# Attention, mixing and gating on one Trainium2 core: the two-bank score tile becomes two tiles of a bank

## The chip, the cores and the metric

The kernel runs on one core of a Trainium2 chip. The metric is the device time of one execution in microseconds, as the median of three runs. The engines are named as the profile names them: PE (TensorE, matmuls), PEld (its weight loads), DVE (VectorE), ACT (ScalarE), POOL (GpSimd) and SP (the queue that issues most DMAs).

## What is computed

Three stages follow each other. The change touches the first alone: attention for 4 batches of 8 heads, 576 positions of 64 features, with a mask in blocks of 64.

```python
scores = scale * np.matmul(q, k.transpose(0, 1, 3, 2))
mask = block_i >= block_j                      # block = 64 positions
scores = np.where(mask, scores, -1000000000.0)
scores = scores - np.max(scores, axis=-1, keepdims=True)
attn = np.exp(scores)
attn = attn / (np.sum(attn, axis=-1, keepdims=True) + 1e-09)
return np.matmul(attn, v).astype(np.float32)
```

The second stage (`_moe_ref`) mixes each position with the one before it and applies three weight matrices; its matmuls write the tiles M. The third (`_moe2_ref`) is a gated layer that mixes positions with a 576 x 576 matrix. All data are float32.

## The kernel before

**Stages and units.** Attention is cut into units. A unit "D" is the low part of one head: queries 0 to 255. A unit "H" is a pair of heads: queries 256 to 511 of each, and the 64 last queries of both heads together, the *tail*, which see all 576 keys. The order (L800) is 16 D units of batches 0 and 1, their 8 H units, then 16 D and 8 H units of batches 2 and 3. The second stage's matmuls (`moe1`, L1295) are woven in between by a schedule of shares (L1375 to L1450), and from about 430 us on the third stage follows alone. In the time line the D units of batches 0 and 1 lie in the first 62 us, the H units of batches 0 and 1 up to about 225 us, the D units of batches 2 and 3 up to about 282 us, and their H units up to about 425 us.

**Scores.** Every unit writes its scores into PSUM. `low_S` (L910) uses 384 columns (128 and 256) of one bank, S0 for even units and S1 for odd ones (for the first four also two tiles M). `high_S` (L1002), called for each head of a pair, writes 384 columns into S0 and 512 into S1. `tail_S` (L1024) writes 576 columns, 288 into the end of the first bank and 288 into the start of the second, so that one instruction can read all 576 side by side. S0 and S1 are the two halves of one tile `sbig` of 1024 columns, which is two banks (L710, L711).

**Softmax.** `soft` (L880) takes a list of parts, each with a column index `c`, the scores in PSUM and the place of the result. For each part DVE copies the scores times -0.125 and keeps the minimum in `nb[:, c]` (`red`, L886), and then ACT takes the exponential from PSUM with that as its bias and adds up the row in `sums` (`exp`, L891). `inverse` (L900) adds the sum and a small constant and takes the reciprocal, and `scaled` (L904) multiplies the probabilities. They are then transposed by TensorE into the tiles T (two tiles of a bank, T0 and T1, L712), and ACT and DVE read them out as a high and a low part (PH, PL) for the product with the values (tiles O0 and O1).

In the profile the first half of an fp32 matmul and the second are two records. P is the probabilities of all parts but the tail, whose tile is Pt.

**How the order is set.** No instruction is emitted where it is written. `nc` is a planner (class `Plan`, L324): every operation is noted with what it reads and writes, and `play` (L402) lays the operations out engine by engine in the order of a modelled time, taking the ready operation of the highest rank. `emit` (L572) then hands them in that order to the framework, which sets the semaphores. For a tile in PSUM the planner notes which banks each operation touches, and lets two engines' operations follow each other where they share a bank (L353 to L360):

```python
lo, hi = x.off // 512, (x.off + sum(st * (n - 1) for st, n in x.dims)) // 512
```

`mm` (L677) also makes the first matmul of a group wait for the last matmul of the group before it in the same tile. `ptile` (L647) hands out a PSUM tile by its tag. Before it reuses one, `order.need` lets the reads of the last use come first in the program's order; `BANKS` (L661) extends this from S to S0 and S1 and back. Where the planner expects TensorE to stand idle in the attention stage, it lays in matmuls on zeros (`calm`, into O0).

All instructions go through `emit` and so carry line 582 in the profile; they are told apart by the names of their tiles.

Of the kernel before, what the change touches and what calls it, by code (L numbers as in the profile page):

```python
# [9 lines left out]
F32 = mybir.dt.float32  # L10
F32R = mybir.dt.float32r
I32 = mybir.dt.int32
AF = mybir.ActivationFunctionType
ALU = mybir.AluOpType
AX = mybir.AxisListType
# [3 lines left out]
B, H, S = 4, 8, 576  # L19
DM = 512  # L20
HF = S // 2
# [8 lines left out]
class Order:  # L30
# [12 lines left out]
    def pe(self, ns):  # L43
        self.run(self.t)
        self.t += ns

    def at(self, dt, fn, *keys):

        heapq.heappush(self.heap, (self.t + dt, self.n, fn))
        for k in keys:  # L50
            self.due[k] = max(self.due.get(k, 0.0), self.t + dt)
        self.n += 1
# [576 lines left out]
def fused_kernel(ctx: ExitStack, tc: tile.TileContext, low, high, tails, mu,  # L629
                 w_k, w_v, w_r, w_in, g_ln, w_sgT, b_sg, w_out, outT):  # L630
    nc = plan = Plan(tc)
# [3 lines left out]
    order = Order()  # L635
# [5 lines left out]
    def pool(name, **kw):  # L641
        p = Pool(plan, name, **kw)
        return p, p

    ring = {}

    def ptile(tag, cols, bufs):  # L647

        r = ring.setdefault(tag, [])
        if len(r) >= bufs:  # L650
            order.need(r[-bufs])
        key = ("ps", tag, len(r))
        r.append(key)
        if tag in fixed:
            t = fixed[tag][(len(r) - 1) % bufs]
            for x in BANKS.get(tag, ()):
                order.need(*ring.get(x, ())[-2:])
            return t, key
        return ps([128, cols], F32, tag, bufs), key

    BANKS = dict(S=("S0", "S1"), S0=("S",), S1=("S",))  # L661


    att_over = []
# [1 line left out]
    def mtile1(w):  # L666
        if att_over:
            tag = att_over[0]
            att_over.append(att_over.pop(0))
        else:  # L670
            tag = "M"
        t, key = ptile(tag, 512, PS_BUFS[tag])
        return t[:, 0:w], key
# [3 lines left out]
    def mm(out, lhsT, rhs, start=False, stop=False):  # L677
        op = nc.tensor.matmul(out=out, lhsT=lhsT, rhs=rhs, start=start, stop=stop)
        t = out.tile
        if start and t in stopped:  # L680
            op.preds[stopped[t].n] = stopped[t]
        if stop:
            stopped[t] = op
# [10 lines left out]
    def sub(who, out, a, b):  # L694
# [12 lines left out]
    x2d = [dram([4, 128, S], F32, f"x2d{b}") for b in range(B)]  # L707

    pcm, ps = pool("ps1", space=PSUM)
    out_ps, sbig = [ps([128, 512], F32, f"O{i}") for i in range(2)], ps([128, 1024], F32, "S")  # L710
    fixed = dict(O=out_ps, S=[sbig], S0=[sbig[:, 0:512]], S1=[sbig[:, 512:1024]],  # L711
                 T=[ps([128, 512], F32, f"T{i}") for i in range(2)])  # L712
    plan.fill(1500.0, "tensor", "matmul", out=out_ps[0][0:64, 512 - FILL:512], lhsT=calm[:, 0:64], rhs=calm, start=True, stop=True)
    mcm, mtile = pool("moe1")
    acm, atile = pool("attn", side="right")

    sums = atile([128, 4, 5, 2], F32, "sums")
    nc.gpsimd.memset(sums[:, :, :, 1], 1e-9)
    ssum = [sums[:, i] for i in range(4)]
    junk = atile([128, 8], F32, "junk")  # L720

# [41 lines left out]
    def w_pair(key, scale, ptile):  # L763

        v = w1[key]
        hi, lo = w1[key] = ptile()
        nc.scalar.activation(out=hi, in_=v, func=AF.Copy, scale=scale)
        if scale != 1.0:
            nc.vector.scalar_tensor_tensor(out=lo, in0=v, scalar=scale, in1=hi.bitcast(F32),
                                           op0=ALU.mult, op1=ALU.subtract)  # L770
        else:
            sub("wl", lo, v, hi.bitcast(F32))
# [107 lines left out]
    def soft(n, parts, normal):  # L880

        sm = ssum[n % 4]
        nb = atile([128, 5], F32, "nb", 4)
        keys = [k for *_, ks in parts for k in ks]

        def red():  # L886
            for c, st, p, _ in parts:
                nc.vector.tensor_scalar(out=p, in0=st, scalar1=-0.125, scalar2=None, op0=ALU.mult, op1=ALU.min,
                                        accum_out=nb[:, c:c + 1])

        def exp():  # L891
            for c, st, p, _ in parts:
                nc.scalar.activation(out=p, in_=st, func=AF.Exp, scale=0.125, bias=nb[:, c:c + 1], accum_out=sm[:, c, 0:1])

        w = sum(st.cols for _, st, _, _ in parts)
        at(0, plan.rank(SB, red), *keys)
        at(1.1 * w + 100, plan.rank(SB, exp), *keys, ("P", n))
        at(2.3 * w + 500, plan.rank(SB, normal), ("P", n))

    def inverse(n, cs, rr):  # L900
        nc.vector.tensor_reduce(out=rr[:, cs], in_=ssum[n % 4][:, cs], axis=AX.X, op=ALU.add)
        nc.vector.reciprocal(out=rr[:, cs], in_=rr[:, cs])

    def scaled(p, r):  # L904
        plan.add(*[("scalar", "activation", dict(out=p, in_=p, func=AF.Copy, scale=r)) if w == "A" else
                   ("vector", "tensor_scalar", dict(out=p, in0=p, scalar1=r, scalar2=None, op0=ALU.mult,
                                                    op1=ALU.add, accum_out=junk[:, 0:1]))
                   for w in WHO["P"]])

    def low_S(n):  # L910
        q, k, v = raws[n]
        tag = SEATS[n] if n < len(SEATS) else f"S{n % 2}"
        st, key = ptile(tag, 512, PS_BUFS[tag])
        p = probs[n] = atile([128, 384], F32, "P2", P2_BUFS)
        pe(4 * 384 / 2.4 + 8)
        parts = []
        b, h = units[n][1:]
        order.need(("sp", n))
        for c, (o, e) in enumerate(((0, 128), (128, 256))):
            qs = slice(128 * c, 128 * c + 128)  # L920
            if b in SCORE_PAIRS:
                Q, K = splits[n]
                mm(st[:, o:o + e], Q[:, qs], K[:, 0:e], start=True)
                mm(st[:, o:o + e], q2[h % 2][:, qs], k2[h % 2][:, LOW:LOW + e], stop=True)
            else:
                mm(st[:, o:o + e], q[:, qs], k[:, 0:e], start=True, stop=True)
            parts.append((c, st[:, o:o + e], p[:, o:o + e], [key]))
        splits.pop(n, None)
        rr = scales[n] = atile([128, 5], F32, "rr", 4)

        def normal():
            inverse(n, slice(0, 2), rr)
            if b in VALUE_PAIRS:
                for c, _, pc, _ in parts:
                    scaled(pc, rr[:, c:c + 1])

        soft(n, parts, normal)
# [64 lines left out]
    def high_S(n, x):  # L1002
        order.need(("sp", n, x))
        Q, K = splits.pop((n, x))
        (s0, k0), (s1, k1) = ptile("S0", 512, 1), ptile("S1", 512, 1)
        p = probs[n, x] = atile([128, 384], F32, "P2", P2_BUFS), atile([128, 512], F32, "P3", P3_BUFS)
        pe(2 * (cost(384) + cost(512)))
        parts = []
        for c, (st, key, e) in enumerate(((s0, k0, 384), (s1, k1, 512))):
            mm(st[:, 0:e], Q[:, 128 * c:128 * c + 128], K[:, 0:e], start=True)  # L1010
            mm(st[:, 0:e], q2[x][:, 128 * c:128 * c + 128], k2[x][:, 0:e], stop=True)
            parts.append((2 * x + c, st[:, 0:e], p[c], [key]))
        if not x:
            scales[n] = atile([128, 5], F32, "rr", 4)
        rr = scales[n]

        def normal():
            inverse(n, slice(2 * x, 2 * x + 2), rr)
            for c in range(2):
                scaled(p[c], rr[:, 2 * x + c:2 * x + c + 1])  # L1020

        soft(n, parts, normal)

    def tail_S(n):  # L1024
        k, q = raws.pop((n, "t"))
        st, key = ptile("S", 1024, 1)
        st = st[:, 512 - HF:512 + HF]
        p = probs[n, "t"] = atile([128, S], F32, "Pt", PT_BUFS)
        pe(8 * HF / 2.4 + 8)
        for i in range(2):  # L1030
            mm(st[:, HF * i:HF * i + HF], q, k[:, HF * i:HF * i + HF], start=True, stop=True)
        rr = scales.pop(n)

        def normal():
            inverse(n, slice(4, 5), rr)
            scaled(p, rr[:, 4:5])

        soft(n, [(4, st, p, [key])], normal)

    def high_T(n, j):  # L1040
        order.need(("P", n))
# [71 lines left out]
    def fronts(n):  # L1113
        if units[n][0] == "D":
            return [lambda: low_S(n)]
        return [lambda: high_S(n, 0), lambda: high_S(n, 1), lambda: tail_S(n)]
# [250 lines left out]
    k = 0  # L1367
# [52 lines left out]
    for i, x in moe1():  # L1420
# [5 lines left out]
        i = ready  # L1426
# [23 lines left out]
        if x > STARTS[-2] + X0_AT * (STARTS[-1] - STARTS[-2]) and not XHL:  # L1450
            XHL[0] = wtile([128, 2, 4, S], F32R, "XHL")
            for f, tag in enumerate(("xh", "xl")):
                t = mtile([128, 4, HF], F32, tag, 2)
# [5 lines left out]
    pcm, ps = pool("ps2", space=PSUM, after=[pcm])  # L1459
# [280 lines left out]
```

## Time and profile before

| what | value |
|---|---|
| median of 3 runs | 707.8 us (707.37 to 709.29) |
| profiled execution | 706.74 us |
| its span (first to last instruction) | 705.0 us |
| PE busy | 681.0 us, 97% of the span |
| PEld busy | 622.6 us, 88% |
| DVE busy | 472.4 us, 67% |
| ACT busy | 420.4 us, 60% |
| POOL busy | 259.2 us, 37% |
| chain that ended last | PE 79%, DVE 7%, ACT 7% |

A busy share is an average over stretches with different limits, so the stretches have to be looked at one by one. Idle time of an engine counts where that engine sets the end. A matmul's end is modelled, and matmuls run one into the other, so PE's busy time also holds some time in which it did less than it could. A line such as "PE S <- ACT P" says that PE stood idle before an instruction that writes S, until an instruction of ACT that writes P had ended.

### The profile page before, as it was taken

The numbers are of one execution on the slowest core, as the hardware profiler recorded it, in microseconds if no ns is written. First come the engines' busy times: TensorE is split into PE (matmuls) and PEld (weight loads), VectorE is DVE, ScalarE is ACT, GpSimd is POOL, SyncE is SP. The second block draws the span as 40 slices with busy tenths as digits, with TensorE's granted clock in tenths as the row PEclk, the third lists the DMA queues.
The fourth block names the chain that finished last, engine by engine and source line by source line (L and its number), as shares of the span: only waits on it lengthen the run. The fifth ranks groups of instructions, "written<-read, shape, count | busy, mean of one in ns | idle before, by whom it ended". The sixth has DMA issues, their size and how long they took to land.

```text
span 705.0 us, 12415 instructions
## 1 busy us (share of the span) xinstructions
PE 681.0 (97%) x4321; PEld 622.6 (88%) x4321; DVE 472.4 (67%) x1321; ACT 420.4 (60%) x1057; POOL 259.2 (37%) x289
## 2 busy tenths in 40 slices
PE   8898999999999888899999999999999999999998
PEld 7777878788999777798999999999898998998997
DVE  4785889777777776687788875771898256346233
ACT  5788786767975787779977886680552132032120
POOL 3004556537741433645645452340235032022031
PEclk9999999999999999999999999999999999999999
DMA  8848132332222222432323214221910400400102
GB/s 309 271 129 287 33 93 83 102 96 68 80 72 82 65 58 87 128 123 82 109 85 120 86 53 155 82 67 46 341 45 4 132 1 0 135 2 6 62 1 68
DMA packets 37403, 67.84 MB, mean 96 GB/s; under 512 B 6564, under 2 KB 21924, under 8 KB 37340
## 3 DMA queue, kind: packets, MB, share of 16 engines
q1 hardware_dynamic: 37196, 67.04, 29.1%
q8 instruction: 34, 0.56, 0.3%
q14 instruction: 29, 0.24, 0.1%
q10 hardware_dynamic: 144, 0.00, 0.0%
HBM read 55.50 MB, written 9.44 MB: 92 GB/s over the span
## 4 chain that ended last, share of the span: by engine, by line
PE 79%; DVE 7%; ACT 7%; DMA 2%; issue 2%; POOL 1%; SPq 0%; ACTq 0%; POOLq 0%; DVEq 0%
PE M L582 37%; PE O L582 16%; PE S L582 12%; PE T L582 7%; PE V L582 7%; ACT P L582 4%; DVE P L582 3%; DVE wv L582 1%; DMA qkv<-high_dram 1%; DVE Pt L582 1%; DVE xT L582 1%; ACT V L582 1%; ACT otmp L582 1%; ACT R L582 1%; DMA q<-Q 1%
## 5 line engine op out<-in xcount | busy, mean ns | idle before, releaser
L582 DVE TENSOR_SCALAR_CACHE_REDUCE P<-S 128x128 f32<-128x128 f32 (+2 forms) x124 | 60.3, 492 | 41.2 <-PE S L582 19.7
L582 PE MATMUL M<-xh,wv 128*128 128x256 f32 (+2 forms) x320 | 85.6, 368 | 0.2
L582 ACT ACTIVATE P<-S,nb 128x128 f32<-128x128 f32 (+2 forms) x124 | 65.3, 528 | 33.4 <-DVE P L582 17.7
L582 DVE TENSOR_TENSOR PL<-T,PH 128x384 fp32r<-128x384 f32 (+1 forms) x128 | 63.2, 505 | 29.0 <-ACT PH L582 23.4
L582 ACT ACTIVATE PH<-T 128x384 fp32r<-128x384 f32 (+3 forms) x152 | 65.2, 432 | 25.6 <-PE T L582 23.4
L582 PE MATMUL M<-xh,w 128*128 128x384 f32 (+1 forms) x272 | 77.6, 340 | 0.0
L582 PE MATMUL M<-kh,wv 128*128 128x320 f32 (+2 forms) x256 | 71.4, 347 | 0.0
L582 PE MATMUL T<-ident,P 128*128 128x128 f32 x320 | 68.8, 279 | 2.4 <-ACT P L582 0.7
L582 POOL TENSOR_TENSOR gt<-gt,U 128x288 f32<-128x288 f32 x32 | 30.9, 970 | 105.7 <-DVE gt L582 55.0
L582 PEld LDWEIGHTS M<-xh,wv 128*128 128x128 f32 x320 | 57.2, 193 | 4.3 <-ACT kl L582 0.3
L582 POOL TENSOR_TENSOR kl<-R,kh 128x384 fp32r<-128x384 f32 (+1 forms) x40 | 41.7, 1044 | 47.3 <-ACT kh L582 45.0
L582 POOL TENSOR_TENSOR xl<-t,xh 128x384 fp32r<-128x384 f32 (+1 forms) x40 | 38.9, 978 | 52.0 <-ACT xh L582 51.7
L582 DVE TENSOR_SCALAR_CACHE_REDUCE P<-P,rr 128x384 f32<-128x384 f32 (+1 forms) x96 | 56.1, 584 | 1.0
L582 ACT ACTIVATE U<-M 128x288 f32<-128x288 f32 x32 | 13.2, 412 | 71.6 <-PE M L582 71.6
L582 PEld LDWEIGHTS T<-ident,P 128*128 128x128 f32 x320 | 42.3, 141 | 13.5 <-DVE P L582 3.4
L582 PE MATMUL O<-gh,w 128*128 128x288 f32 x256 | 52.1, 296 | 0.1
L582 PE MATMUL M<-XHL,w 128*128 128x288 f32 x384 | 51.7, 295 | 0.0
L582 PEld LDWEIGHTS M<-XHL,w 128*128 128x128 f32 x384 | 51.2, 188 | 0.1
L582 PEld LDWEIGHTS M<-xh,w 128*128 128x128 f32 x272 | 49.2, 190 | 1.1
L582 POOL TENSOR_TENSOR V<-qkv,V 128x320 fp32r<-128x320 f32 (+1 forms) x48 | 35.0, 741 | 40.4 <-ACT V L582 35.8
L582 PE MATMUL O<-PH,V 128*128 128x320 f32 (+3 forms) x192 | 48.6, 305 | 0.7 <-ACT PH L582 0.5
L582 PE MATMUL M<-kl,wv 128*128 128x256 f32 (+2 forms) x160 | 47.6, 350 | 0.0
(214 smaller groups left out, 1899.7 us busy)
## 6 DMA issues: line engine op xcount, KB each, us to landing
qkv<-high_dram SPq DMA_DIRECT2D x32, 544.0 KB
tail<-tails_dram SPq DMA_DIRECT2D x16, 352.0 KB
X<-x2d SPq DMA_DIRECT2D x4, 1152.0 KB
outT_dram<-o SPq DMA_DIRECT2D x32, 144.0 KB
w<-w_k_dram SPq DMA_DIRECT2D x4, 1024.0 KB
w<-w_v_dram SPq DMA_DIRECT2D x4, 1024.0 KB
w<-w_in_dram SPq DMA_DIRECT2D x4, 1024.0 KB
qkv<-low_dram SPq DMA_DIRECT2D x20, 132.0 KB
```

What stands on the lines that cost most here:

```text
L582: getattr(getattr(self.nc, e), fn)(*pos, **{k: real(x) for k, x in a.items() if k[0] != "_"})
```

## The change

S0 and S1 become two PSUM tiles of 512 columns, and the tile of 1024 columns goes, with the table `BANKS` and its `order.need`. `tail_S` writes 288 columns at the start of each of the two. Its softmax has two parts for one, with column indices 4 and 5: two reductions, a minimum of the two results into column 4, two exponentials that both take column 4 as their bias, and two row sums, which `inverse` adds up together. `nb` and `sums` get a sixth column, and the small constant of the sixth is zero, with a memset of its own.

```diff
--- before.py
+++ after.py
@@ -653,12 +653,8 @@
         r.append(key)
         if tag in fixed:
             t = fixed[tag][(len(r) - 1) % bufs]
-            for x in BANKS.get(tag, ()):
-                order.need(*ring.get(x, ())[-2:])
             return t, key
         return ps([128, cols], F32, tag, bufs), key
-
-    BANKS = dict(S=("S0", "S1"), S0=("S",), S1=("S",))
 
 
     att_over = []
@@ -707,15 +703,16 @@
     x2d = [dram([4, 128, S], F32, f"x2d{b}") for b in range(B)]
 
     pcm, ps = pool("ps1", space=PSUM)
-    out_ps, sbig = [ps([128, 512], F32, f"O{i}") for i in range(2)], ps([128, 1024], F32, "S")
-    fixed = dict(O=out_ps, S=[sbig], S0=[sbig[:, 0:512]], S1=[sbig[:, 512:1024]],
+    out_ps = [ps([128, 512], F32, f"O{i}") for i in range(2)]
+    fixed = dict(O=out_ps, S0=[ps([128, 512], F32, "S0")], S1=[ps([128, 512], F32, "S1")],
                  T=[ps([128, 512], F32, f"T{i}") for i in range(2)])
     plan.fill(1500.0, "tensor", "matmul", out=out_ps[0][0:64, 512 - FILL:512], lhsT=calm[:, 0:64], rhs=calm, start=True, stop=True)
     mcm, mtile = pool("moe1")
     acm, atile = pool("attn", side="right")
 
-    sums = atile([128, 4, 5, 2], F32, "sums")
-    nc.gpsimd.memset(sums[:, :, :, 1], 1e-9)
+    sums = atile([128, 4, 6, 2], F32, "sums")
+    nc.gpsimd.memset(sums[:, :, 0:5, 1], 1e-9)
+    nc.gpsimd.memset(sums[:, :, 5, 1], 0.0)
     ssum = [sums[:, i] for i in range(4)]
     junk = atile([128, 8], F32, "junk")
 
@@ -880,17 +877,22 @@
     def soft(n, parts, normal):
 
         sm = ssum[n % 4]
-        nb = atile([128, 5], F32, "nb", 4)
+        nb = atile([128, 6], F32, "nb", 4)
         keys = [k for *_, ks in parts for k in ks]
+
+        halves = parts[0][0] == 4
 
         def red():
             for c, st, p, _ in parts:
                 nc.vector.tensor_scalar(out=p, in0=st, scalar1=-0.125, scalar2=None, op0=ALU.mult, op1=ALU.min,
                                         accum_out=nb[:, c:c + 1])
+            if halves:
+                nc.vector.tensor_tensor(out=nb[:, 4:5], in0=nb[:, 4:5], in1=nb[:, 5:6], op=ALU.min)
 
         def exp():
             for c, st, p, _ in parts:
-                nc.scalar.activation(out=p, in_=st, func=AF.Exp, scale=0.125, bias=nb[:, c:c + 1], accum_out=sm[:, c, 0:1])
+                d = min(c, 4)
+                nc.scalar.activation(out=p, in_=st, func=AF.Exp, scale=0.125, bias=nb[:, d:d + 1], accum_out=sm[:, c, 0:1])
 
         w = sum(st.cols for _, st, _, _ in parts)
         at(0, plan.rank(SB, red), *keys)
@@ -898,7 +900,8 @@
         at(2.3 * w + 500, plan.rank(SB, normal), ("P", n))
 
     def inverse(n, cs, rr):
-        nc.vector.tensor_reduce(out=rr[:, cs], in_=ssum[n % 4][:, cs], axis=AX.X, op=ALU.add)
+        x = ssum[n % 4][:, cs] if cs.start < 4 else ssum[n % 4][:, 4:6].rearrange("p (a c) t -> p a (c t)", a=1)
+        nc.vector.tensor_reduce(out=rr[:, cs], in_=x, axis=AX.X, op=ALU.add)
         nc.vector.reciprocal(out=rr[:, cs], in_=rr[:, cs])
 
     def scaled(p, r):
@@ -1023,19 +1026,21 @@
 
     def tail_S(n):
         k, q = raws.pop((n, "t"))
-        st, key = ptile("S", 1024, 1)
-        st = st[:, 512 - HF:512 + HF]
         p = probs[n, "t"] = atile([128, S], F32, "Pt", PT_BUFS)
         pe(8 * HF / 2.4 + 8)
+        parts = []
         for i in range(2):
-            mm(st[:, HF * i:HF * i + HF], q, k[:, HF * i:HF * i + HF], start=True, stop=True)
+            st, key = ptile(f"S{i}", 512, 1)
+            hs = slice(HF * i, HF * i + HF)
+            mm(st[:, 0:HF], q, k[:, hs], start=True, stop=True)
+            parts.append((4 + i, st[:, 0:HF], p[:, hs], [key]))
         rr = scales.pop(n)
 
         def normal():
             inverse(n, slice(4, 5), rr)
             scaled(p, rr[:, 4:5])
 
-        soft(n, [(4, st, p, [key])], normal)
+        soft(n, parts, normal)
 
     def high_T(n, j):
         order.need(("P", n))
```

## Rows read from the trace of the kernel before

**Rows 1.** stretches, us; PE, PEld, DVE, ACT, POOL busy us (instructions); clock; DMA; GB/s
```profile
0.00:75.00 75.00, 65.55 (x473) 55.39 (x474) 48.67 (x166) 53.93 (x146) 16.55 (x36) 0.98 0.71 236
75.00:225.00 150.00, 148.10 (x866) 127.38 (x865) 118.28 (x338) 111.50 (x284) 77.99 (x72) 1.00 0.25 80
225.00:300.00 75.00, 65.97 (x412) 57.70 (x412) 53.55 (x226) 58.85 (x181) 31.18 (x46) 1.00 0.29 87
300.00:425.00 125.00, 124.78 (x761) 115.26 (x761) 101.04 (x305) 107.71 (x278) 67.54 (x69) 1.00 0.29 93
425.00:705.00 280.00, 276.55 (x1816) 266.85 (x1815) 150.88 (x289) 88.39 (x172) 65.90 (x67) 1.00 0.21 71
175.00:200.00 25.00, 24.92 (x172) 23.20 (x171) 19.39 (x61) 24.39 (x66) 17.93 (x23) 1.00 0.34 113
```

**Rows 2.** TensorE's waits, 0 to 75 us: total us, times, longest
```profile
PE S L582 <- ACT P L582: 3.4, 5, 1.0
PE S L582 <- DVE P L582: 1.8, 3, 0.7
```

**Rows 3.** TensorE's waits, 225 to 300 us
```profile
PE S L582 <- ACT P L582: 5.3, 12, 0.8
PE S L582 <- DVE P L582: 2.5, 5, 0.7
```

**Rows 4.** timeline, first high heads: start, us, engine, operation [idle before <-ended by]
```profile
65.78 0.50 PE L582 MATMUL S<-k,q 128*128 128x512 f32 x1 [0.66 <-DVE P L582]
...
69.40 0.56 DVE L582 TENSOR_SCALAR_CACHE_REDUCE P<-S 128x384 f32<-128x384 f32 x1 [0.82 <-PE S L582]
...
70.02 0.50 PE L582 MATMUL S<-k,q 128*128 128x512 f32 x1 [0.66 <-DVE P L582]
...
70.56 0.58 ACT L582 ACTIVATE P<-S,nb 128x384 f32<-128x384 f32 x1 [0.46 <-PE S L582]
```

**Rows 5.** timeline in the low heads of batch 2
```profile
236.94 0.47 ACT L582 ACTIVATE P<-S,nb 128x256 f32<-128x256 f32 x1
...
237.54 0.92 PE L582 MATMUL S<-qkv 66*128 66x128 f32 x4 [0.20 <-ACT P L582]
...
241.26 0.42 DVE L582 TENSOR_SCALAR_CACHE_REDUCE P<-S 128x256 f32<-128x256 f32 x1 [0.57 <-PE S L582]
...
241.75 0.70 PE L582 MATMUL S<-qkv 66*128 66x256 f32 x2 [0.53 <-DVE P L582]
```

**Rows 6.** timeline, the transposes' tiles T in the same stretch
```profile
252.53 0.56 DVE L582 TENSOR_TENSOR PL<-T,PH 128x384 fp32r<-128x384 f32 x1
...
252.66 0.27 PE L582 MATMUL T<-ident,P 128*128 128x128 f32 x1
```

**Rows 7.** stretches around the fall of the granted clock, as rows 1
```profile
64.00:69.00 5.00, 3.35 (x32) 2.49 (x29) 1.46 (x6) 3.36 (x10) 2.99 (x4) 1.00 0.84 255
...
70.30:73.90 3.60, 3.60 (x17) 3.09 (x16) 3.31 (x11) 1.80 (x5) 2.08 (x3) 0.53 0.12 26
```

**Rows 8.** groups by form: count | busy us, mean ns | idle before
```profile
L582 ACT ACTIVATE P<-S,nb 128x256 f32<-128x256 f32 x30 | 14.2, 472 | 8.9 <-PE S L582 6.3 <-DVE P L582 2.6
...
L582 DVE TENSOR_SCALAR_CACHE_REDUCE P<-S 128x256 f32<-128x256 f32 x30 | 12.5, 417 | 5.3 <-ACT P L582 3.4 <-PE S L582 1.8
...
L582 DVE TENSOR_REDUCE rr<-sums 128x2 f32<-128x4 f32 x64 | 9.9, 155 | 20.2 <-ACT P L582 19.3
...
L582 DVE TENSOR_SCALAR_CACHE_REDUCE Pt<-S 128x576 f32<-128x576 f32 x16 | 12.0, 749 | 1.0 <-PE S L582 0.9
L582 ACT ACTIVATE Pt<-S,nb 128x576 f32<-128x576 f32 x16 | 11.8, 737 | 4.5 <-DVE Pt L582 4.4
...
L582 ACT ACTIVATION_READ_ACCUMULATOR Pt<-S,nb 128x1 f32 x16 | 3.1, 192 | 0.0
```

**Rows 9.** waits of the whole run, the weight loads ahead of S
```profile
PEld S L582 <- ACT P L582: 14.6, 30, 1.1
...
PEld S L582 <- DVE P L582: 6.9, 9, 1.0
```

## The prediction

> **What bounds the kernel now.** I read the table of stretches first [rows 1]. From 425 us on TensorE is busy for 276.6 of 280 us (most of the rest is the last output's way out) and in the last attention stretch (300 to 425) for 124.8 of 125, so whatever TensorE loses ahead of that is lost to the end. It loses it in two places: 9.5 us of idle in the first 75 us and 9.0 us between 225 and 300, where the low halves (units of kind "D") of batches 2 and 3 run. DVE (53.6 of 75) and ACT (58.9 of 75) are not full there.
>
> The list of TensorE's waits says for what it stands idle: for the score tile S. Ended by ACT's or DVE's work on P, it is 5.2 us in the first 75 us [rows 2] and 7.8 us in 225 to 300 [rows 3]. P is written from S, so at first sight the bank is simply not read out yet.
>
> The timeline tells more. At 69.40 DVE reduces the 384 columns of S0; the matmul that adds into the 512 columns of S1 starts at 70.02, as that reduction ends, after 0.66 us of idle; and ACT's exponential of S0, whose maximum has been there since 69.96, starts at 70.56, when the matmul into the *other* bank is through [rows 4]. In a low stretch the same: the unit whose scores went in at 237.54 sits in one bank. The next unit's bank was read for the last time by the exponential of 236.94, yet its second matmul waits until 241.75, for the reduction at 241.26, which reads the first unit's bank [rows 5]. So S0 and S1 take turns as if they were one buffer: a write waits for reads that were issued ahead of it in either bank, and a read for writes in either bank. In no stretch that I read does a read of S lie over a write of S. The tiles T0 and T1, which are separate tiles of a bank each, do not behave so: DVE reads T at 252.53 for 0.56 us while a transpose into T starts at 252.66 [rows 6]. The kernel's own planner keeps books by bank (L353 to L359), so its order counts on an overlap that the tile does not give. I conclude that the semaphores are set by tile, and S is one tile of two banks.
>
> **What the change removes.** With two tiles, a wait for the other bank has no ground left.
>
> *Stretch 225 to 300.* TensorE's idle before S is 5.3 + 2.5 = 7.8 us [rows 3]. Below, the change gives nothing there; above, it also gives back what the weight loads stood still (below, under the rivals). Can it be had whole? The stretch would shrink to some 67 us, and ACT's 58.9 us would fill 88% of it. In 175 to 200 ACT is 98% full and TensorE still gets 24.9 of 25 us; in 300 to 425 ACT is 86% full and TensorE gets 99.8% [rows 1]. These rows are nearer than any other, so I take the whole: **-7.8 us**.
>
> *First 75 us.* Of the 5.2 us [rows 2], the waits at 65.78 and 70.02, 0.66 us each [rows 4], and between them the longest of those that ACT ended, 1.0 us, come in a row at the first high heads: 2.3 together. I take them whole. The other 2.9 us lie in the low heads of batches 0 and 1, where the order also carries zero matmuls that the planner lays into gaps it expects, and where DVE rebuilds weights. Ends: 0 and 2.9; I take half, 1.4, since no row says which of the two binds once the wait is gone. Together **-3.7 us**.
>
> *The clock.* From 70.3 to 73.9 us TensorE's granted clock is 0.53 on average, so it ran nearly the whole of it at 1.2 GHz and not at 2.4. In 64 to 69, just ahead, TensorE was busy for 3.35 of 5 us [rows 7], and the three waits of 2.3 us fall into that and the following microsecond. Without them it is as busy as elsewhere, where the clock stays at 1.00 [rows 1]. If it stays here, 3.6 x 0.47 = 1.7 us are saved; if not, nothing. I take **-1.7 us**.
>
> *High heads, 75 to 225 and 300 to 425.* TensorE's idle is 1.9 + 0.2 us in all [rows 1], little of it before S: I put **-0.4 us**.
>
> **What it adds.** Sixteen tails each become two halves of 288 columns. TensorE's work is the same: the tail was two matmuls of 288 columns already. ACT has two exponentials for one: the 576 wide takes 737 ns and the 256 wide 472 [rows 8], that is 0.83 ns a column, so 288 take some 498, and two take 259 ns more than one; with a second read of the accumulator (192 ns) it is 0.45 us. DVE: 749 ns against 417 for 256 columns gives 1.04 ns a column, 450 for 288, so 151 more. The minimum over the two halves is one more small instruction; the nearest is the reduction of two or four sums, 155 ns. With a second accumulator read, which the ACT figure bounds from above at 0.19, that is 0.3 to 0.5 us. Sixteen times: 7.2 us of ACT, at most 8 us of DVE. Behind the minimum, which waits for both halves, the scaling of the last scores and the subtractions PL stand in DVE's queue, and behind the exponentials the evictions PH; the transposes wait for these. What hides all this is TensorE's other work, the M matmuls: in the high stretches TensorE waits for almost nothing while ACT is at 111.5 of 150 and 107.7 of 125 us [rows 1]. Where the cover is thin is 175 to 200, with ACT at 24.4 of 25: one or two tails there put 0.45 us each in the way. Ends: a small gain (the first half can be reduced while the second is multiplied) and 15 us, all on the path; I take **+0.5 us**.
>
> The Trainium skill speaks against this part: "Perfetto Trace Analysis", Optimizing Scalar/DVE Operations, says that every instruction pays an access overhead and that larger operations raise the throughput of an engine that is saturated. By that rule the 0.5 would be 7.2 if ACT were full throughout, which the rows show for a single stretch of 25 us.
>
> One more memset on POOL (busy 16.6 of the first 75 us [rows 1]) and a sum over four values instead of two I put at nothing: POOL's and DVE's own slack hides them. No DMA is added or moved, and no queue is passed. The added instructions shift the planner's list a little; no row gives that a sign, and it goes into the range.
>
> **Sum.** -7.8 - 3.7 - 1.7 - 0.4 + 0.5 = -13.1 us. The profiled execution took 706.74 us (span 705.0), so 693.6. The median of the runs is 707.8, 1.1 more: 694.7, and I write **695.0 us**, -1.8%.
>
> **Rivals.**
>
> *Half comes back as another wait.* Once S is free the next late thing is the chain exponential, normalisation, transpose. In 225 to 300 ACT is the fullest of the helpers, and its queue is in order: an exponential waits behind evictions. Then half of the 7.8 and 3.7 us returns and the clock still falls: 707.8 - 5.8 = 702.0 us. For it: 88% of ACT in the compressed stretch. Against it: the two stretches with ACT at 86% and 98%.
>
> *More than the idle comes back.* Weight loads before S stood still for 14.6 + 6.9 = 21.5 us over the run [rows 9], 8.1 us more than the 13.4 us of TensorE's idle (5.2, 7.8 and 0.4 above). A modelled matmul end hides the start of a stall. If all of that is real, the sum is 8 us lower: 687 us. Against it: a load that waits costs nothing while matmuls ahead of it still run. The Trainium skill ("Perfetto Trace Analysis", Identifying the Most-Contended Engine) holds that the busy share of the matmuls is a bad measure, since they are pipelined, and that of the weight loads a good one; by it this rival is the forecast. Weight loads take 57.7 of 75 us in 225 to 300 and 115.3 of 125 in 300 to 425 [rows 1], but the mix of matmul widths differs too, so I don't take the difference as loss.
>
> *The waits stay, and it is slower.* If the turns that S0 and S1 take come from elsewhere than the shared tile (the pool, or the order in which the engines' instructions were laid), nothing is removed. Then each tail's added instructions lie in a chain that is already serial, from its scores to the transposes: up to 0.45 + 0.5 us each, 15 us for sixteen, 723 us at the full price. It decides as soon as more than two of the sixteen are uncovered (2 us is what can be told from no change); with a quarter of them, 711.5 us. With none, the time stays at 708: the change then does not do what it says. Against both: the separate tiles T0 and T1 overlap [rows 6].
>
> **How the numbers follow.** The forecast (689 to 699 us) gets 0.60, half coming back (699 to 705) 0.19, more than the idle (684 to 689) 0.08, the waits staying 0.13: 0.06 with no change, 0.07 slower. A measurement of this kernel tells some 0.3%, 2.1 us, from no change. Faster is 0.60 + 0.19 + 0.08 = 0.87. The range leaves out the slower cases, no change and part of the best: 687 to 704 us. Its ends are also the bounds of the terms: 687 with the weight loads' figure, 704 with 4 us left of the 13.
>
> **What would show it.** In the profile after: reads of S0 that lie over writes of S1 (right) or still none (wrong from the root); TensorE's idle before S in 225 to 300 down from 7.8 us to below 2; idle in that stretch from 9.0 to below 3, or else a new name, T or O, in the list of waits (the first rival); the granted clock at 1.00 in 64 to 75 (the third term); ACT and DVE instructions on Pt doubled, with TensorE's busy share in the high stretches unchanged (the added part). A total above 705 us would make the prediction wrong.

## The result, and the profile after

The changed kernel takes 678.3 us (677.4 to 682.6, four runs), the kernel before in the same session 708.4 (707.4 to 709.3). The ratio is 0.9587, interval 0.9544 to 0.9630. The forecast was 695.0 with a range of 687 to 704: the sign and the cause were right, the gain of 30.2 us is more than twice the forecast's 13.1, and the time lies below the range.

First the page of the kernel after: span, busy times, and the shares of the chain that ended last.

```profile
span 676.6 us, 12475 instructions
...
PE 669.4 (99%) x4320; PEld 617.4 (91%) x4320; DVE 469.7 (69%) x1369; ACT 419.9 (62%) x1089; POOL 258.3 (38%) x290
...
PE 88%; ACT 4%; DVE 3%; DMA 2%; POOL 1%; issue 1%; SPq 0%; POOLq 0%; ACTq 0%
```

TensorE's busy time was 681.0 us in a span of 705.0. Its idle time fell from 24.0 to 7.2 us, that is by 16.8, and its busy time by 11.6, though its matmuls are the same but for one on zeros. A forecast made from idle alone could not see the second figure.

The stretches, in the columns of [rows 1], and behind them the two around the fall of the clock [rows 7]:

```profile
0.00:75.00 75.00, 72.99 (x539) 63.33 (x540) 58.27 (x194) 62.82 (x174) 22.16 (x41) 1.00 0.71 242
75.00:225.00 150.00, 148.95 (x898) 129.04 (x897) 121.37 (x391) 115.25 (x311) 77.20 (x80) 1.00 0.27 86
225.00:300.00 75.00, 74.78 (x493) 69.99 (x492) 60.64 (x238) 68.11 (x206) 41.53 (x50) 1.00 0.33 99
300.00:425.00 125.00, 124.54 (x750) 116.05 (x750) 94.09 (x287) 99.67 (x258) 58.10 (x60) 1.00 0.32 107
...
64.00:69.00 5.00, 5.00 (x27) 3.97 (x27) 4.86 (x16) 3.95 (x13) 2.59 (x3) 1.00 0.30 83
69.00:75.00 6.00, 6.00 (x36) 4.99 (x35) 5.09 (x10) 5.06 (x14) 3.59 (x3) 1.00 0.06 12
```

The first 75 us hold 2.0 us of idle instead of 9.5, and 225 to 300 holds 0.2 instead of 9.0, with 493 matmuls in the same 75 us where there were 412. The clock stays at 1.00.

All of TensorE's waits of the whole run, then the longest of its weight loads':

```profile
PE O L582 <- POOL calm L582: 1.2, 1, 1.2
PE S L582 <- DMA q<-Q: 0.9, 2, 0.5
PE S L582 <- POOL Q L582: 0.4, 1, 0.4
```

```profile
PEld S L582 <- ACT P L582: 4.0, 13, 0.5
PEld O L582 <- ACT PH L582: 4.0, 14, 0.5
PEld S L582 <- issue: 3.9, 12, 0.7
PEld T L582 <- DVE P L582: 2.2, 10, 0.3
...
PEld T L582 <- DVE PL L582: 0.9, 4, 0.3
```

The waits on P ahead of S [rows 2, 3] are gone from the first list, and of the 21.5 us in which the weight loads ahead of S stood [rows 9] 4.0 are left.

The timeline at the first high heads answers to [rows 4]. The 384 columns are in S0, the 512 in S1:

```profile
59.06 0.50 PE L582 MATMUL S<-K,Q 128*128 128x512 f32 x1
59.15 0.56 DVE L582 TENSOR_SCALAR_CACHE_REDUCE P<-S 128x384 f32<-128x384 f32 x1
...
59.40 0.39 PE L582 MATMUL S<-k,q 128*128 128x512 f32 x1
```

DVE reads S0 from 59.15 to 59.71, and both matmuls into S1 run beside it. Counted over the trace, 69 of 318 reads of S (the reductions and exponentials, and six of the later stages) lie over a write of S, for 21.9 us together; before, none of 286 did.

Last the operations on the tail, which were one of 576 columns each [rows 8], and the new minimum (the second view gives least, median and most, in ns):

```profile
L582 ACT ACTIVATE Pt<-S,nb 128x288 f32<-128x288 f32 x32 | 15.9, 500 | 9.6 <-DVE nb L582 9.6
L582 DVE TENSOR_SCALAR_CACHE_REDUCE Pt<-S 128x288 f32<-128x288 f32 x32 | 14.5, 452 | 0.5 <-PE S L582 0.5
...
L582 ACT ACTIVATION_READ_ACCUMULATOR Pt<-S,nb 128x1 f32 x32 | 6.4, 201 | 0.0
```

```profile
L582 DVE TENSOR_TENSOR nb<-nb x16: 145/154/601, 65.9 to 395.7; 128x1 f32<-128x1 f32 x16
```

The estimates were 498, 450 and 155 ns.

### The profile page after: what moved, and what is told of

It reads as the page before. It is cut to its first block, busy times and chain, and to the rows that moved or that the text cites. A ratio compares the mean times of both kernels' runs of the same rounds, so it can differ in the third digit from the quotient of the medians.

```text
span 676.6 us, 12475 instructions
## 1 busy us (share of the span) xinstructions
PE 669.4 (99%) x4320; PEld 617.4 (91%) x4320; DVE 469.7 (69%) x1369; ACT 419.9 (62%) x1089; POOL 258.3 (38%) x290
## 4 chain that ended last, share of the span: by engine, by line
PE 88%; ACT 4%; DVE 3%; DMA 2%; POOL 1%; issue 1%; SPq 0%; POOLq 0%; ACTq 0%
PE M L582 43%; PE O L582 18%; PE S L582 12%; PE T L582 8%; PE V L582 7%; ACT P L582 1%; DMA qkv<-high_dram 1%; DMA q<-Q 1%; ACT PH L582 1%; DVE P L582 1%; DVE wv L582 1%; ACT wv L582 1%; POOL k L582 1%; POOL Q L582 0%; DVE PL L582 0%
## 5 line engine op out<-in xcount | busy, mean ns | idle before, releaser
L582 ACT ACTIVATE PH<-T 128x384 fp32r<-128x384 f32 (+3 forms) x152 | 65.7, 433 | 28.4 <-PE T L582 24.5
L582 DVE TENSOR_SCALAR_CACHE_REDUCE P<-S 128x128 f32<-128x128 f32 (+2 forms) x124 | 59.7, 490 | 17.8 <-PE S L582 11.6
L582 PE MATMUL M<-kh,wv 128*128 128x320 f32 (+2 forms) x256 | 69.4, 345 | 0.0
L582 PE MATMUL M<-kl,wv 128*128 128x256 f32 (+2 forms) x160 | 49.1, 348 | 0.0
L582 PE MATMUL O<-PH,V 128*128 128x320 f32 (+3 forms) x192 | 46.8, 301 | 0.1
```

The source lines that it names most:

```text
L582: getattr(getattr(self.nc, e), fn)(*pos, **{k: real(x) for k, x in a.items() if k[0] != "_"})
```

## The experiments

The change has three parts: the tail is computed in halves, the banks become tiles of their own, and the planner, which now knows both, writes another order. Half of the kernels below hold the order fixed and change what is emitted, so that one part is seen alone.

### 1. The tile alone, in the order of after

The kernel after, its plan untouched; at emission the two score tiles are views of one tile of two banks. TensorE's 4320 matmuls come in the same order as in the kernel after.

```diff
+    joint = ps([128, 1024], F32, "S")
+    for i in range(2):
+        fixed[f"S{i}"][0].make = joint[:, 512 * i:512 * i + 512].make
```

> The changed kernel, its plan and the halves of the tail kept, but S0 and S1 are again views of one PSUM tile of two banks when the instructions are emitted; the order on every engine stays that of the changed kernel. Theory A (semaphores are set by tile, and the waits on the other bank are the whole of the gain): 704 to 713 us, with TensorE's idle before S back at 10 us or more and the granted clock falling again near 70 us. Theory B (the gain comes from another order of the work that the planner finds for two tiles): within 3 us of the changed kernel, 675 to 681 us. Theory C (the gain comes from the halves of the tail): the same, 675 to 681 us.

Measured: 720.3 us, ratio 1.0174 (1.0130 to 1.0219). In this order the tile alone is worth 42 us, and without it the change would have been slower than before. The time lies above the range of each of the three theories: the cause is that of A, and its price was put too low. In the trace none of 318 reads of S lies over a write of S. Its page, TensorE's waits and the first stretch:

```profile
span 723.1 us, 12492 instructions
...
PE 689.0 (95%) x4320; PEld 624.1 (86%) x4320; DVE 473.1 (65%) x1369; ACT 424.7 (59%) x1089; POOL 257.7 (36%) x290
```

```profile
PE S L582 <- ACT P L582: 9.3, 18, 1.2
PE S L582 <- ACT Pt L582: 5.8, 11, 0.7
PE S L582 <- DVE P L582: 4.8, 11, 0.7
```

```profile
0.00:75.00 75.00, 65.26 (x451) 56.09 (x451) 45.02 (x154) 51.55 (x140) 13.85 (x34) 0.91 0.71 234
```

The waits before S that end on P or Pt are back, 19.9 us of them. Against the profile after, with the same matmuls in the same order, the span is 46.5 us longer: 26.9 of it is idle (34.1 against 7.2) and 19.6 shows as busy time (689.0 against 669.4). Part of the latter is the clock, whose mean in the first 75 us is 0.91, that is at most 0.09 x 75 = 6.8 us there. The profiled execution was the slowest of the four (724.8 us, the others 719.6 to 721.0), so the 46.5 us are more than the 42 of the medians.

### 2. The same done to the transposes' tiles

If the turns come from tiles of several banks and not from anything about S, then T0 and T1, which overlapped before [rows 6], must start to take turns once they are one tile.

```diff
+    joint = ps([128, 1024], F32, "T")
+    for i in range(2):
+        fixed["T"][i].make = joint[:, 512 * i:512 * i + 512].make
```

> The changed kernel, but the two tiles T of the transposes are views of one PSUM tile of two banks, with the plan unchanged. Theory A (any two-bank PSUM tile makes the banks take turns): slower, 685 to 705 us, since reads of T lie over writes of T for 15 us of the changed kernel's trace, and no read of T lies over a write of T afterwards. Rival (the turns were particular to S, whose tail was read over both banks): no change, 677 to 680 us.

Measured: 701.5 us, ratio 0.9902 (0.9863 to 0.9941), 23 us above the kernel after. Its page, TensorE's waits and its weight loads':

```profile
span 698.6 us, 12482 instructions
...
PE 679.2 (97%) x4320; PEld 616.5 (88%) x4320; DVE 471.4 (67%) x1369; ACT 421.5 (60%) x1089; POOL 258.4 (37%) x290
```

```profile
PE T L582 <- ACT PH L582: 7.9, 20, 0.6
PE T L582 <- DVE PL L582: 3.5, 6, 1.7
```

```profile
PEld T L582 <- ACT PH L582: 16.1, 27, 0.9
PEld T L582 <- DVE PL L582: 9.1, 21, 2.0
```

PH and PL are the evictions of T. No read of T lies over a write of T any more; in the kernel after 46 of 318 did, for 10.7 us (the 15 us of the expectation count a read once for each write under it). The idle that TensorE shows ahead of T is 11.4 us, the loads' standing time 25.2, and the loss 23: the loads tell the size, the idle tells half.

### 3 and 4. The order of before, with one tile and with two

Both keep the planner's picture of the kernel before, a tail of 576 columns in one piece, so TensorE's 4321 matmuls stand in the order of before. At emission the tail's reduction, exponential and sum are replaced by those of two halves. In the first the halves lie in the shared tile, in the second in two tiles.

```diff
+            if op.expand:
+                op.expand()
+                continue
...
+                if c == 4:
+                    op.expand = lambda: [tc.nc.scalar.activation(
+                        out=p[:, hs[i]].make(), in_=banked(i), func=AF.Exp, scale=0.125, bias=col[0].make(),
+                        accum_out=sm[:, 4 + i, 0:1].make()) for i in range(2)]
```

The second differs from the first by:

```diff
-        return sbig[:, 512 - HF + HF * i:512 + HF * i].make()
+        return single[i][:, 0:HF].make()
+    single = [ps([128, 512], F32, f"S{i}") for i in range(2)]
+    for i in range(2):
+        fixed[f"S{i}"][0].make = single[i].make
```

> The kernel before with its plan, its two-bank tile and its order on every engine; only at emission each of the tail's instructions becomes its halves (two reductions and a minimum, two exponentials, a sum over four). Theory A1 (in a chain where the banks take turns the halves cost time of their own, and are what makes the one-tile kernel with the new plan slower than the kernel before): 716 to 723 us. Theory A2 (the 12 us come from the new plan): 707 to 712 us.

> As e5_old_plan_one_tile, with S0 and S1 as two tiles of a bank at emission; the plan stays that of the kernel before. Theory A (the two tiles alone are worth some 40 us at a given order): 676 to 684 us. Theory B (a good part of the gain comes from the planner's new order): 688 to 700 us.

Measured: one tile 712.8 us, ratio 1.0077 (1.0041 to 1.0114); two tiles 686.2 us, ratio 0.9692 (0.9662 to 0.9722). On this chip the kernel before took 708.35. So halves without separate tiles cost 4.5 us, the tiles give back 26.6, and what the new order adds is the rest of the way to after. The first lies just above the range of A2, so of the 12 us by which experiment 1 was slower than before, 4.5 are the halves and the rest goes with the new order; the second lies between the ranges of its two theories. The pages, each with TensorE's longest waits behind it:

```profile
span 709.8 us, 12498 instructions
...
PE 683.9 (96%) x4321; PEld 622.0 (88%) x4321; DVE 477.0 (67%) x1369; ACT 423.7 (60%) x1089; POOL 259.7 (37%) x290
```

```profile
PE S L586 <- ACT P L586: 8.7, 17, 1.0
PE S L586 <- DVE P L586: 4.3, 8, 0.7
```

```profile
span 683.8 us, 12481 instructions
...
PE 672.2 (98%) x4321; PEld 619.1 (91%) x4321; DVE 478.6 (70%) x1369; ACT 420.8 (62%) x1089; POOL 259.8 (38%) x290
```

```profile
PE T L586 <- DVE PL L586: 2.3, 4, 1.7
PE T L586 <- DVE P L586: 1.7, 4, 0.7
```

The waits before S that end on P are gone, 60 of 318 reads of S lie over a write of S where with one tile none did, and the longest waits that are left are 4.0 us for DVE ahead of T. Again about half of the 26.0 us of span shows as idle (25.9 to 11.6, 14.3 us) and the rest, 11.7 us, as busy time of the same matmuls.

### 5 and 6. The second half's reduction and the minimum left out

This asks what the tail's added DVE work costs. The first kernel takes it out of the plan, the second only at emission, so that its order is that of after.

```diff
-            for c, st, p, _ in parts:
+            for c, st, p, _ in parts[:1] if halves else parts:
...
-            if halves:
-                nc.vector.tensor_tensor(out=nb[:, 4:5], in0=nb[:, 4:5], in1=nb[:, 5:6], op=ALU.min)
```

```diff
+                if c == 5:
+                    op.expand = lambda: None
...
-                nc.vector.tensor_tensor(out=nb[:, 4:5], in0=nb[:, 4:5], in1=nb[:, 5:6], op=ALU.min)
+                nc.vector.tensor_tensor(out=nb[:, 4:5], in0=nb[:, 4:5], in1=nb[:, 5:6], op=ALU.min).expand = lambda: None
```

> The changed kernel without the reduction of the tail's second half and without the minimum over the halves: both exponentials take the first half's minimum as their bias. It leaves out the maximum over the second half's keys. It takes away 16 x (0.45 + about 0.15) us of DVE's work and the wait of the first exponential for the second half. My prediction's term (the tail's added work is hidden, 0.5 us): 676.5 to 679 us. Rival (the tails' added work lies on the path): 668 to 674 us.

> The changed kernel with its plan; at emission the reduction of the tail's second half and the minimum over the halves are left out, so the maximum over the second half's keys is missing. As e3_no_second_min, but with the order of everything else unchanged. If the 4 us that e3_no_second_min was slower came from its plan alone: 675 to 678.5 us here, that is no more than 3 us of gain, since the tail's added work is hidden. If the added work lies on the path: 668 to 674 us.

Measured: 682.5 us replanned, ratio 0.9629 (0.9597 to 0.9661); 678.25 in the order of after, ratio 0.9590 (0.9559 to 0.9621). The first is 4 us *slower* with less work, which neither theory had, though its interval overlaps that of the kernel after; the second equals the kernel after. So the added DVE instructions cost nothing where they stand, and what the first is slower by goes with its new order. The second exponential was not taken out in any run.

### 7. Four separate tiles for the sums

If every shared tile made its users take turns, the tile `sums`, whose four slices serve four units, would too.

```diff
+    own = [atile([128, 6, 2], F32, f"sums{i}") for i in range(4)]
...
+    for i in range(4):
+        ssum[i].make = own[i].make
```

> The changed kernel with its plan; the row sums, one SBUF tile that all units share in four slots, become four tiles at emission. Theory A for PSUM alone (the turns belong to tiles of several PSUM banks; an SBUF tile is followed by regions): no change, 676 to 680 us. Theory A for every tile (any shared tile makes its readers and writers take turns): faster, below 675 us.

Measured: 678.3 us, ratio 0.9583 (0.9553 to 0.9613): no effect. This shared tile, in SBUF, costs nothing here.

### 8 to 12. Where the new order's gain comes from

In the planner, `mm` makes the first matmul of a group wait for the last of the group before in the same tile. With one tile that tied S0's groups to S1's; with two the tie is gone. Number 8 puts the tie back into the kernel after. Number 9 takes it out of the kernel of experiment 4, whose planner still sees the tail whole. Numbers 10 to 12 move a constant of the planner, the 20 ns that it adds to each operation that isn't TensorE's, by half a nanosecond: that asks how much of a difference is mere chance of the order.

```diff
         t = out.tile
+        t = fixed["S0"][0].tile if "S1" in fixed and t is fixed["S1"][0].tile else t
```

```diff
-        t = out.tile
+        t = (out.tile, out.off // 512) if out.tile is sbig.tile else out.tile
```

```diff
-MORE = 20.0
+MORE = 19.5
```

Number 10 has the last edit alone, number 11 the same with 20.5, and number 12 has 19.5 together with the tie of number 8.

> The changed kernel, with two tiles, but the planner again makes the first matmul of a group in S0 or S1 wait for the end of the group before it in either. Theory A (the order does not matter): 676 to 681 us. Theory B (the gain comes from the freer order): above 685 us.

> As e6_old_plan_two_tiles, but the planner no longer makes the first matmul of a group in S0 or S1 wait for the end of the group before it in the other bank. Theory P1 (this tie is what the new plan gained 8 us by): 675 to 682 us. Theory P2 (the 8 us are chance of the plan, which any small edit moves by several us): anywhere from 677 to 690 us, and no nearer to 678 than to 686.

> The changed kernel, with the planner's allowance per instruction (MORE) at 19.5 ns and not 20, which alters nothing but the order. Theory P1: within 3 us of the changed kernel, 675 to 681.5 us. Theory P2: as likely 682 to 690 us.

> The changed kernel, with the planner's allowance per instruction (MORE) at 20.5 ns and not 20. Theory P1: 675 to 681.5 us. Theory P2: as likely 682 to 690 us.

> e4_shared_order (the changed kernel with the tie back in the planner) with MORE at 19.5 ns. Theory P1: 683 to 690 us, as the other two tied plans (686.0 and 686.2). Theory P2: anywhere from 677 to 690 us.

| planner sees the tail | tie | time, us | ratio, interval |
|---|---|---|---|
| in halves | no (after) | 678.3 | 0.9587 (0.9544 to 0.9630) |
| in halves | no, 19.5 | 680.4 | 0.9610 (0.9582 to 0.9639) |
| in halves | no, 20.5 | 679.4 | 0.9598 (0.9572 to 0.9625) |
| in halves | yes (no. 8) | 686.0 | 0.9685 (0.9646 to 0.9724) |
| in halves | yes, 19.5 (no. 12) | 684.0 | 0.9661 (0.9631 to 0.9692) |
| whole | yes (exp. 4) | 686.2 | 0.9692 (0.9662 to 0.9722) |
| whole | no (no. 9) | 686.2 | 0.9689 (0.9658 to 0.9720) |

The plans that differ by half a nanosecond lie up to 2 us apart, with intervals that overlap, so differences of that size say nothing. The untied, halved plans lie between 678.3 and 680.4, the four others between 684.0 and 686.2. Dropping the tie gives nothing while the planner sees the tail whole (number 9, for which P1 had 675 to 682 us; the other four came out in the ranges of B and P1; the two executions of number 9 at a clock of 1.00 took 684.4 and 684.8), and seeing the halves gives 0 to 2 us while the tie stands. Together they are worth 7.9 us at the constant 20 (686.2 to 678.3), where the intervals are apart. At 19.5 dropping the tie is worth 3.6 (684.0 to 680.4), and there the intervals touch, so how much of the 7.9 is a lucky order stays open. A planner that sees the tail whole also keeps the table `BANKS`; no run separates the two.

What differs shows in part in the weight loads ahead of T, of experiment 4 and, below, of number 8:

```profile
PEld T L586 <- DVE P L586: 7.6, 20, 1.0
PEld T L586 <- DVE PL L586: 6.0, 13, 2.1
...
PEld T L586 <- DVE Pt L586: 2.4, 7, 0.5
```

```profile
PEld T L582 <- DVE P L582: 3.5, 14, 0.3
PEld T L582 <- DVE PL L582: 3.3, 10, 0.6
```

Experiment 4 has 16.0 us and number 9 15.7, against 3.1 in the profile after. A planner that doesn't know that a tail takes DVE two reductions and a minimum may lay the transposes too early; that is argued from these rows, and no run changed it alone. It isn't the whole either: numbers 8 and 12, whose planner sees the halves, have 6.8 and 5.1 us of such waits and are about as slow. In number 8 TensorE waits for other things, such as a DMA of q ahead of S (2.1 us) and ACT's PH and PL ahead of O (3.2 us).

## Why the prediction was right about the cause and wrong about the size

The same landmarks in the four traces that matter, from the view of the tile S (start of the first or last matmul of a kind, us). For the kernel before and after its lines are:

```profile
L582 PE MATMUL S<-qkv x80: 272/378/483, 40.4 to 279.3; 66*128 66x128 f32 x40, 66*128 66x256 f32 x40
L582 PE MATMUL S<-K,Q x64: 334/412/524, 62.2 to 414.8; 128*128 128x384 f32 x32, 128*128 128x512 f32 x32
...
L582 PE MATMUL S<-tail x64: 403/406/510, 73.9 to 418.4; 128*128 128x288 f32 x64
```

```profile
L582 PE MATMUL S<-qkv x80: 272/370/463, 34.7 to 255.3; 66*128 66x128 f32 x40, 66*128 66x256 f32 x40
L582 PE MATMUL S<-K,Q x64: 333/412/578, 53.8 to 389.1; 128*128 128x384 f32 x32, 128*128 128x512 f32 x32
...
L582 PE MATMUL S<-tail x64: 403/406/510, 61.6 to 392.5; 128*128 128x288 f32 x64
```

| section, us | before | halves, one tile (exp. 3) | halves, two tiles (exp. 4) | after | before to after | forecast |
|---|---|---|---|---|---|---|
| start to first high head | 62.2 | 62.3 | 53.9 | 53.8 | -8.4 | -1.4 |
| to first tail | 11.7 | 11.9 | 7.5 | 7.8 | -3.9 | -4.0 |
| to last low score | 205.4 | 207.2 | 196.3 | 193.7 | -11.7 | -7.8 and most of -0.4 |
| to last tail | 139.1 | 141.7 | 139.2 | 137.2 | -1.9 | rest of -0.4 |
| to the end | 286.6 | 286.7 | 286.9 | 284.1 | -2.5 | 0 |
| span | 705.0 | 709.8 | 683.8 | 676.6 | -28.4 | -13.1 with the tail's +0.5 |

**The cause** stands. With matmuls in one and the same order, making S two tiles takes 26.6 us away in the order of before and 42 in that of after; the reads now lie over the writes; and joining T brings the same kind of wait. "The waits stay, and it is slower" was the wrong rival, but its price was not idle: with one tile, halves are slower by 4.5 us, near a third of the 15 that it put on sixteen tails, and in the order of after by 12.

**The size of the tile's term is the step that failed.** The sum priced the tile by the idle that TensorE shows ahead of S, in the first 62 us by half of that, and put what else the turns cost, the clock apart, at nothing. From before to experiment 4, which has the old order, the span falls by 21.2 us. TensorE's idle accounts for 12.4 of these (24.0 to 11.6); the other 8.8 stood in the trace as busy time of the same matmuls, of which the clock is 1.7.

The first 62 us show what else was missed: 1.4 us were counted on, and 8.3 came back. TensorE's idle fell there by 5.6 us, and only 2.9 of it lay ahead of S. Most of the rest lay ahead of T and O, in the kernel before:

```profile
PE O L582 <- DVE otmp L582: 1.1, 1, 1.1
...
PE T L582 <- ACT P L582: 0.7, 2, 0.4
PE T L582 <- ACT xT L582: 0.7, 1, 0.7
```

These don't name S, so the sum left them out. But the idle of this section behind its first matmul is 6.0 us in the kernel before and in experiment 3, and 0.4 in experiment 4, so the tiles alone remove them. A read of S waited for a write of the other bank as well [rows 4], and what comes behind that read was late with it; that this is the way is argued.

The rival "more than the idle comes back" was right in kind: it had 21.5 us from [rows 9], and its 687 stands beside the measured 686.2. That it comes so near is in part luck. It set its 8.1 us on a sum that held 11.9 of the 13.4 us that it had subtracted. In experiment 4 the loads still stand 3.0 us ahead of S for P and 8.7 us longer ahead of T for DVE (16.0 against 7.3), and in the first 62 us they had stood 4.4 us ahead of S, where 8.3 came back. Its counter-argument, that a waiting load costs nothing while matmuls ahead of it run, isn't borne out: more came back than TensorE's idle. The Trainium skill, "Perfetto Trace Analysis", Identifying the Most-Contended Engine, holds matmul busy time to be a poor measure of headroom and the weight loads' a good one. These traces agree: the time in which no load ran fell by 17.7 us from before to experiment 4 (82.4 to 64.7) and by 23.2 to after (59.2), TensorE's idle by 12.4 and 16.8, and the span by 21.2 and 28.4.

**225 to 300 us**: the waits went whole, and in the kernel after no other took their place in TensorE's list. The rival "half comes back" fell: ACT, 68.1 of 75 us busy there, holds nothing up. In experiment 4, in the old order, it was right in a small part: T did come as a new name, with 2.1 us of waits for DVE in this stretch. Up to the last low score 9.1 us went from before to experiment 4 (7.8 and most of 0.4 forecast), and another 2.6 by the order.

**First high heads and the clock**: forecast -2.3 and -1.7, measured -3.9 together, with the clock at 1.00. Right, and not by luck: from before to experiment 4 TensorE's idle in this section falls by 2.1 us, and the clock stays at 1.00.

**The tail's added work**, +0.5: nothing speaks against it in the kernel after, where leaving its DVE part out changes nothing (678.25 against 678.3); its ACT part was not left out alone. The Trainium skill, "Perfetto Trace Analysis", Optimizing Scalar/DVE Operations, would have larger operations where the engine is saturated. ACT has two exponentials of 500 ns for one of 737, and in the stretches with tails it is busy for 115.3 of 150 and 99.7 of 125 us, so it isn't saturated there, and no run here shows that price. The cost of the halves depends on the tiles: in experiment 3 the section that holds half of the tails is 2.6 us longer than before, and in experiment 4 it is back to 139.2.

**The order**, "shifts a little; no row gives that a sign", was put at nothing. This is the second step that failed. The order is worth 7.9 us here (686.2 to 678.3), or 3.6 by the pair at the other constant. The first step alone brings the time to 686.2, just below the range, and the second takes it well out. Of the 7.2 us of span between experiment 4 and after, 2.8 lie behind the last tail (286.9 to 284.1), and what sets these stays open. The tie in `mm` bore on it, which bound the two banks in the planner too; the working named the planner's books by bank and left the tie out.

**What would show it**: the reads over writes, the idle before S (below 2; now 0), the idle in 225 to 300 (below 3; now 0.2), the clock, and the doubled instructions on Pt with TensorE's share in the high stretches unchanged (148.95 of 150 and 124.54 of 125) all came out as listed.

## What to carry to other kernels

Where a PSUM tile spans several banks that are used in turns, look in the timeline for a read of one bank over a write of another; if there is none, give each bank a tile of its own, and split the one instruction that reads across. To size such a wait, take the weight loads' standing time as well as TensorE's idle, count the idle ahead of the tiles further down the chain too, and let the range reach beyond all of these. When an order is computed from the dependences, ask which of them the change removes in the planner as well, and test parts of the change in a fixed order, since a new order by itself was worth up to 8 us here.

## What was not expected of the hardware

A stall of TensorE shows up in part as busy time. In three pairs with identical matmuls in identical order, TensorE's idle took 14.3 of 26.0 us of span (experiments 3 and 4), 26.9 of 46.5 (after and 1, some of that the clock) and 12.2 of 22.0 (after and 2). The time in which no weight load ran came nearer in all three: 23.1, 39.8 and 22.9 us.

Where the rest went can be read from the third pair, in which the clock stays at 1.00. The records of matmuls lie over each other: the 4320 of the kernel after add up to 1383 us in 669 us of busy time. Of the 9.8 us that don't show as idle, 6.3 are consecutive records that overlap less, and 3.5 are records drawn longer.

The granted clock fell where TensorE had just stood: it was busy for 3.35 of 5 us ahead of the fall in the kernel before [rows 7], for 5.04 of 7.6 us ahead of 17.6 us in experiment 1, and for 2.48 of 4.8 us ahead of 58.6 us in number 9. The mean of the first 75 us is 0.98 before [rows 1], 0.91 in experiment 1, which has the most waits, and 1.00 after. No run changed the clock alone.
